# A gated pair of state-space convolutions: the sequence split as 64 rows at stride 32 instead of 32 rows at stride 64, with the transforms in quarter tiles of the matmul array

## The chip, the cores and the metric

The kernel runs on one core of a Trainium2 chip, in float32. The metric is the device time of one execution in microseconds. The core's engines run side by side, each in its own order: TensorE (matmuls, PE in the profile; PEld are its weight loads), VectorE (DVE), ScalarE (ACT), GpSimd (POOL) and SyncE (SP), which issues the transfers. Matmuls read SBUF and write PSUM.

## The reference

Two state-space layers, A and B, are run over the same input and mixed by a gate. Each is a long convolution: a kernel K of 2048 samples for each of 512 channels, made from 128 complex modes, and a causal convolution by a transform of twice the length.

```python
def _A_ref(u, A_re, A_im, B_re, B_im, C_re, C_im, log_dt, Dskip):   # B_ref is the same
    dt = jnp.exp(log_dt)[:, None]
    logdA = dt * (A_re + 1j * A_im)
    dB = dt * (B_re + 1j * B_im)
    P = jnp.exp(logdA[:, :, None] * l[None, None, :])               # l = 0 .. 2047
    K = jnp.einsum("dn,dnl,dn->dl", Cc, P, dB).real
    y = irfft(rfft(pad(u)) * rfft(pad(K)))[..., :L]                 # over the sequence
    return y + u * Dskip
x = A_u
g = sigmoid((x * gate_w).sum(-1, keepdims=True))
return g * a + (1 - g) * b                                          # a = A_ref(x, ..), b = B_ref(x, ..)
```

## The kernel before

The 512 channels are worked in 8 chunks of 64; a chunk holds 128 rows, 64 of layer A and 64 of B. The sequence index is split in two, and the transform is done in two matmul steps with a small transform each, over 32 shifted frequencies of 64 values.

Per chunk there are 8 **tables** (`tables`, T = 0 .. 63 in all), each for 16 rows. GpSimd makes angles (`ang`) and most of the magnitudes (`mr`, some on VectorE), ScalarE takes two sines and a square into PSUM (`s`, `sq`), VectorE multiplies them together (`ei`, `mr`, four instructions). `kgen` (L549, L553) then contracts over the 128 modes on TensorE and gives the convolution kernel in the time domain, with Dskip added to its first sample by the small matmuls of L553. A copy takes the result to `kt`. After each second table `first` (L569) does the first step of the transform in 64x64 tiles; two copies take its two banks to `xa` or `xb`, one buffer for a chunk.

The input's own spectra are made once for pairs of chunks (`u_spectra`: `uin` loads, four `first`, eight steps at L592) and spilled to DRAM (`us`). `gated` makes the gate's matrices `gsi` with a matmul (L613), a tanh and a few small operations.

When a chunk's buffer is full, `conv` runs for it in 8 steps (s = 0 .. 63 in all): two loads of the input's spectrum to `u`, four matmuls of the second step on the full array (L652) into the bank `fw`, one VectorE multiply by `u` (L656) to `y`, eight matmuls of the inverse (L665, L666) into a bank of `c`, a copy to `z` and a spill to `zb` in DRAM. The last chunk's steps use `s` and `sq`, free by then, beside `fw`. After a chunk's 8 steps `fin` loads `zb` back transposed (`f`, in the last chunk `ei` and `mr`), does the inverse's last step together with the gate (L694), copies and stores, four times.

What sets the order: every operation is recorded in program order with its engine or engines, and a table of numbers, `ORDER`, gives the sequence in which they are issued; a letter behind a number picks the second engine. Each engine runs its share strictly in that sequence, and so does the one queue of SP. Rings of buffers (3 of `mr`, 2 of `ei`, `ang`, `u`, `y`, `z`, `f`, one `s` and `sq`; three banks of `c`) set how far one engine may run ahead of another. The prologue (`prep`, `spread_dt`, L366) turns the parameters into the tables' seeds, for the first chunk alone and then for the others in two groups.

A matmul of the program shows in the trace as two records, each with its weight load.

Of the kernel before, what the change touches and what calls it, by code (L numbers as in the profile page):

```python
# [16 lines left out]

L, D, NS = 2048, 512, 128
L1, L2 = 32, 64
F1, F2 = 32, 64  # L20
DC = 64
CU = DC // 4
# [3 lines left out]
NG = CH // G  # L26
QK = CH // 4
GROUPS = ((0,), (1, 2, 3), (4, 5, 6, 7))
# [6 lines left out]
ROUND64 = 1.5 * 2.0 ** 17  # L35


def constants():

    f32 = np.float32  # L40
    out = {}
    l1, f1 = np.arange(L1), np.arange(F1)
    ang = 2 * np.pi * ((l1[:, None] * (4 * f1[None, :] + 1)) % 128) / 128
    c, s = np.cos(ang), np.sin(ang)
    w1k = np.zeros((2, 2, L1, 2, F1, 2))
    for q in range(2):
        w1k[:, q, :, 0, :, q] = c
        w1k[:, q, :, 1, :, q] = -s
    si = np.zeros((F1, 2, 2, 2, L1))
    for q in range(2):  # L50
        si[:, 0, q, q, :] = c.T
        si[:, 1, q, q, :] = -s.T
    l2, f2 = np.arange(L2), np.arange(F2)
    k = l2[None, :, None] * (4 * f1[:, None, None] + 1 + 128 * f2[None, None, :])
    ang = 2 * np.pi * (k % 8192) / 8192
    c, s = np.cos(ang), np.sin(ang)
    w2 = np.concatenate([np.concatenate([c, -s], 2), np.concatenate([s, c], 2)], 1)
    out["w2"] = np.ascontiguousarray(w2.transpose(1, 0, 2)).reshape(128, F1 * 128).astype(f32)

    order = np.array([16 * (2 * r + q) + i for q in range(2) for r in range(2) for i in range(16)])  # L60
    ct = c.transpose(0, 2, 1)[:, :, order] / L
    st = s.transpose(0, 2, 1)[:, :, order] / L
    vv = np.concatenate([np.concatenate([ct, st], 2), np.concatenate([-st, ct], 2)], 1)
    vv = np.concatenate([-vv[:, :, 64:], vv], 2)
    out["vv"] = np.ascontiguousarray(vv.transpose(1, 0, 2)).reshape(128, F1 * 192).astype(f32)
    sign = np.repeat([1.0, -1.0], 64)[:, None]
    out["small"] = np.concatenate([w1k.reshape(128, 128), si.reshape(128, 64), si.reshape(128, 64) / 2, si.reshape(128, 64) / 2, np.eye(128), sign, np.ones((128, 128)), np.full((128, 1), math.pi / 4)], 1).astype(f32)
    ints = np.concatenate([2 * np.arange(32) + 1, np.arange(4), 4 * np.arange(8), [-63]])
    out["cint"] = np.broadcast_to(ints.astype(np.int32), (128, 45)).copy()
    return out  # L70
# [9 lines left out]
30 46 31 176 175 334 185 86 47 178 89 48 13 32 77 14 87 4 33 60 59 179 88 181 61 34 78 91 90 92 35b 93 62b 80 51 180 99 52 79  # L80
53b 66b 70 65b 94 186 56 63 101 95 85 57b 213 54 58 67b 55 81b 333 187b 12 96 102 182 372 71 64 72 217 359 184b 188 183 360
201 100 363 195 103 104 97 124 68 106 69 98 361b 110 189 202 73 364 196 203 362b 198 197 116 107 109 192 365 366 115b 120 16
17 373 117 190 417 204 191 111 367 205 368 376 335 206 105 112b 118 108 113 374b 199 377 127 128 369 375 1321 378 126 119 370
379 380 193b 194 74 125 371b 381 75 388 382 114 383 1328 390b 384 123 385 389 76 122 121 391b 392 129 130 164 387 393 207 133
1322 132b 395 386 358 338 131 210 200 208 135 209 134 136 337 145 137 394 139 146 138 396 401 140 403 402 143 405 144 339 404b
147 141 150 142 148 151b 397 154 211 153 160 398 159b 418 408 399 341 409 155 421 156 406 161 152 407 162 163b 157 400 410 342
212 419b 340 166 170 336 214 422 420 411 168 430 423 424 1335 412 1329 431 216 425 221 165 432 426 434 435 427 9 433b 413 436
414 446 437 475 459 215b 438 447 343 439 149 415b 158 440 416b 460 167 1336 461b 428 462 450 344b 346 218 448 225 220 449b 429
171 451 222 219b 476 345 453 452 441 479 169 224 172 442 454 223b 443 480 463 455 477 456 444 445 482 226 466 464 457 228 227b
478 465 467 232 458b 481 468 235 233 483 484 229 469 234 493 470 485 230b 495 487 231 471 486 472 488 236 494 489 241 237 474  # L90
496 473 490 244 497 509 1323 498 242b 500 243 510 491 245 1324 511 499 246 250 501 1342 1330 247 513 502 512 251 522 492b 514
516 517 503 252 238 523 248 1325 515 249 524 253 1331 504 1326b 525 518 1337 505 526 538 1343 1327 519 540 239 506 1338 527
240 1332 1349 529 528 541 1350 1356 1344 530 507 539 531 1339 551 508 542 1345 532 552 543 520 1340 544 1333 533 1357 1377 569
# [54 lines left out]


class Plan:  # L150

    SWITCH = {"act": 1283, "pe": 100}

    def __init__(self, slots):
        self.slots = slots  # L160
# [36 lines left out]
def ssm_mix(ctx: ExitStack, tc: tile.TileContext, a, out, dry=False):  # L197
# [36 lines left out]
    for k in range(4):  # L234
        single["w2", k] = [128, 8, 128]
        single["vv", k] = [128, 8, 192]
# [547 lines left out]
```

## Time and profile before

| what | value |
|---|---|
| three runs | 506.87, 507.98, 508.52 us, median 507.98 |
| profiled execution, first to last instruction | 507.3 us, mean granted TensorE clock 0.946 |
| instructions in the trace | 23,878 |
| moved by DMA | 86.28 MB, mean 170 GB/s |
| HBM read, written | 53.08 MB, 31.65 MB |

The page splits the time by engine (busy time, share of the span), follows the chain of waits back from the last instruction, and groups instructions by line of the program. Busy time of matmuls is modelled from overlapping records, so how fast TensorE gets on is better read from when its records start. "Issue" in the chain is time in which an engine waited for nothing that the profile names. The instructions themselves also come by DMA; they have queues of their own in the page (q8 and q14).

The forty slices of the span, in tenths of each slice:

```profile
PE   2674467698998986999989798899898989899955
DVE  5999899589899986798879869888998889885420
PEclk9987675989999999999999999999999999999997
DMA  8645754835335754455565635445556769642865
```

### The profile page before, as it was taken

The numbers are of one execution on the slowest core, as the hardware profiler recorded it, in microseconds if no ns is written. First come the engines' busy times: TensorE is split into PE (matmuls) and PEld (weight loads), VectorE is DVE, ScalarE is ACT, GpSimd is POOL, SyncE is SP. The second block draws the span as 40 slices with busy tenths as digits, with TensorE's granted clock in tenths as the row PEclk, the third lists the DMA queues.
The fourth block names the chain that finished last, engine by engine and source line by source line (L and its number), as shares of the span: only waits on it lengthen the run. The fifth ranks groups of instructions, "written<-read, shape, count | busy, mean of one in ns | idle before, by whom it ended". The sixth has DMA issues, their size and how long they took to land.

```text
span 507.3 us, 23878 instructions
## 1 busy us (share of the span) xinstructions
PE 420.6 (83%) x10566; PEld 392.4 (77%) x10566; DVE 413.3 (81%) x526; ACT 366.9 (72%) x630; POOL 367.9 (73%) x302
## 2 busy tenths in 40 slices
PE   2674467698998986999989798899898989899955
PEld 2374456598988885898979798898898889799944
DVE  5999899589899986798879869888998889885420
ACT  3982468878799777798986679788988998762200
POOL 1465449989798998789979968799899989830001
PEclk9987675989999999999999999999999999999997
DMA  8645754835335754455565635445556769642865
GB/s 267 235 148 155 239 137 143 300 130 179 97 97 144 215 171 134 132 174 170 152 185 179 189 107 169 150 147 170 151 168 183 216 184 248 173 127 64 241 191 143
DMA packets 90535, 86.28 MB, mean 170 GB/s; under 512 B 6048, under 2 KB 76832, under 8 KB 90432
## 3 DMA queue, kind: packets, MB, share of 16 engines
q1 hardware_dynamic: 90192, 84.10, 55.6%
q8 instruction: 83, 1.36, 1.1%
q0 software_dynamic: 240, 0.66, 0.4%
q14 instruction: 20, 0.16, 0.1%
HBM read 53.08 MB, written 31.65 MB: 167 GB/s over the span
## 4 chain that ended last, share of the span: by engine, by line
PE 54%; DVE 13%; issue 9%; ACT 8%; DMA 7%; SPq 1%; POOL 0%; POOLq 0%; DVEq 0%; ACTq 0%
PE c L665 10%; PE fw L652 9%; PE c L666 9%; PE c L549 9%; PE c L569 7%; PE c L694 4%; PE c L592 3%; DMA zb<-z 3%; DVE ei L283 3%; DVE mr L293 2%; DMA ei<-zb 1%; DVE y L656 1%; ACT sq L296 1%; DMA gsi<-in_par_dram 1%; ACT ml L489 1%
## 5 line engine op out<-in xcount | busy, mean ns | idle before, releaser
L293 DVE SCALAR_TENSOR_TENSOR mr<-sq,mr 128x1024 f32<-128x1024 f32 (+1 forms) x128 | 118.4, 946 | 6.4 <-ACT sq L296 6.2
L283 POOL TENSOR_TENSOR mr<-ml 128x1024 f32<-128x1024 f32 x55 | 108.3, 1972 | 19.5 <-PE c L549 8.3
L665 PE MATMUL c<-y,vv 128*128 128x128 f32 x512 | 103.5, 284 | 1.9 <-DVE xb L308 1.1
L666 PE MATMUL c<-y,vv 128*128 128x128 f32 x512 | 100.7, 279 | 0.0
L283 POOL TENSOR_TENSOR ang<-par,cint 128x512 int32<-128x512 int32 x64 | 69.4, 1084 | 28.9 <-ACT sq L296 23.0
L283 DVE TENSOR_TENSOR ei<-s,mr 128x1024 f32<-128x1024 f32 x64 | 77.8, 1216 | 8.9 <-PE c L553 4.6
L665 PEld LDWEIGHTS c<-y,vv 128*128 128x128 f32 x512 | 79.0, 195 | 3.4 <-DVE xb L308 1.3
L666 PEld LDWEIGHTS c<-y,vv 128*128 128x128 f32 x512 | 79.3, 196 | 0.0
L296 ACT ACTIVATE s<-ang 128x1024 f32<-128x1024 int32 x64 | 65.9, 1030 | 17.5 <-DVE ei L293 8.4
L656 DVE TENSOR_TENSOR y<-fw,u 128x1024 f32<-128x1024 f32 x57 | 69.3, 1215 | 10.2 <-PE fw L652 9.0
L549 PE MATMUL c<-mr 128*32 128x64 f32 x2048 | 67.0, 227 | 11.8 <-DVE mr L293 7.8
L296 ACT ACTIVATE sq<-ang 128x1024 f32<-128x1024 f32 x64 | 65.9, 1030 | 12.4 <-DVE mr L293 11.7
L306 ACT ACTIVATE z<-c 128x512 f32<-128x512 f32 x73 | 43.1, 591 | 38.8 <-PE c L666 27.3
L283 POOL TENSOR_TENSOR ang<-sa 128x512 int32<-128x512 int32 x64 | 70.0, 1095 | 0.4
L296 ACT ACTIVATE ang<-ang 128x1024 f32<-128x1024 int32 x64 | 67.5, 1054 | 0.7
L549 PE MATMUL c<-ei 128*32 128x64 f32 x2048 | 65.5, 225 | 0.3 <-issue 0.3
L549 PEld LDWEIGHTS c<-mr 128*32 128x32 f32 x2048 | 48.9, 113 | 19.4 <-issue 10.6
L283 POOL TENSOR_TENSOR mr<-mh 128x512 f32<-128x512 f32 x58 | 63.6, 1097 | 0.2
L549 PEld LDWEIGHTS c<-ei 128*32 128x32 f32 x2048 | 50.7, 114 | 0.4 <-issue 0.4
L569 PE MATMUL c<-small,kt 64*64 64x64 f32 x2048 | 43.2, 228 | 8.5 <-issue 5.7
L569 PEld LDWEIGHTS c<-small,kt 64*64 64x64 f32 x2048 | 37.0, 140 | 13.0 <-issue 6.6
L569 PE MATMUL c<-small,uin 64*64 64x64 f32 x1024 | 24.9, 243 | 24.1 <-DMA small<-in_small_dram 7.9
(109 smaller groups left out, 759.8 us busy)
## 6 DMA issues: line engine op xcount, KB each, us to landing
zb<-z SPq DMA_DIRECT2D x64, 256.0 KB, 3.3
u<-us SPq DMA_DIRECT2D x114, 128.0 KB, 3.4
f<-zb SPq DMA_DIRECT2D x28, 512.0 KB, 5.0
us<-z SPq DMA_DIRECT2D x32, 256.0 KB, 2.5
uin<-in_uk_dram SPq DMA_DIRECT2D x16, 256.0 KB, 3.8
f<-in_ut_dram SPq DMA_DIRECT2D x8, 512.0 KB, 5.0
out_dram<-o SPq DMA_DIRECT2D x27, 128.0 KB, 2.7
vv<-in_vv_dram SPq DMA_DIRECT2D x4, 768.0 KB, 8.1
```

Of the source, the lines that this page charges most:

```text
L283: op(engs, 0, lambda e: (dve if e == "dve" else pool).tensor_tensor(out=out(), in0=in0(), in1=in1(), op=o), reads, writes, port=port)
L293: lambda _: dve.scalar_tensor_tensor(out=out(), in0=in0(), scalar=s, in1=in1(), op0=o0, op1=o1), reads, writes, port=port)
L296: op("act", c_act(n), lambda _: act.activation(out=out(), in_=in_(), func=func, **{k: v() if callable(v) else v for k, v in kw.items()}), ...
L306: act.activation(out=o(), in_=i(), func=AF.Copy)
L549: pe.matmul(ps[32 * j:32 * j + 32, o, 0:64], x[:, 4 * o + j, 64:96], x[:, 4 * o + j, 0:64], start=o + part == 0, stop=False, tile_position ...
L569: pe.matmul(t(*ps[h]).rearrange("p a b -> p (a b)")[64 * r:64 * r + 64, 64 * g:64 * g + 64], t(*x)[64 * h:64 * h + 64, g], t("small")[64 * ...
L592: pe.matmul(p[:, k], t("w2", j // 2)[:, 4 * (j % 2) + k], t(*x1)[:, 4 * j + k], start=True, stop=True)
L652: pe.matmul(fv()[:, :, k], t("w2", j // 2)[:, 4 * (j % 2) + k], t(*x1)[:, 4 * j + k], start=True, stop=True)
L656: op("dve", 1134, lambda _: dve.tensor_tensor(out=t(*y).rearrange("p h s f d -> p h s (f d)"), in0=fv().rearrange("p s f d -> p s (f d)"). ...
L665: pe.matmul(t(*ps)[:, k], v[:, 64:192], t(*y)[:, 0, :, k], start=True, stop=False)
L666: pe.matmul(t(*ps)[:, k], v[:, 0:128], t(*y)[:, 1, :, k], start=False, stop=True)
L694: pe.matmul(t(*ps)[64 * r:64 * r + 64, i, 0:DC], t("gsi")[:, 4 * k + i, s, 64 * r:64 * r + 64], fv()[:, r, i, DC * s:DC * s + DC], start=s ...
```

## The change

The sequence is split the other way, 64 rows at stride 32, so there are 64 shifted frequencies of 32 values. Every matmul of the transforms now contracts over 64 rows (real and imaginary parts of 32 values, or 64 samples), and the array is used as quarter tiles, two row halves by two column halves, each half of the rows writing a bank of its own.

- `kgen` swaps the operands: 64 + 2 matmuls a table, 32 wide, instead of 32 + 4, 64 and 4 wide.
- `first` has 64 matmuls on 64 rows and 32 columns instead of 32 on 64 rows and 64 columns, still 64 wide.
- the second step (`spectrum`, for the input and for `conv`) handles 16 frequencies in 32 matmuls, 64x64, 64 wide; there were 4 matmuls of 128x128, 128 wide, a step; 8 steps a chunk are now 4.
- the inverse has 32 matmuls, 64x64, 128 wide, in each of 4 steps a chunk, instead of 8 of 128x128 in each of 8.
- `fin` and the gate keep their matmuls.
- VectorE's multiply takes two instructions a step, one a bank; `u` is loaded by one transfer that writes its rows twice; `us` rows are 2 KB, `f` rows 4 KB.
- rings: `c` has 4 single banks and `fw` is gone; `kt` 2, `z` 3, `u` 2.
- `ORDER` is new throughout, and the buffer of a ring is picked by when it comes free. Its rows are numbers:

```diff
-7 0 8 5 82 6 10 11 2 1 173 3 36b 38b 37b 84 83 40b 39b 43 18 177 41b 50 19 42 15 20 21 22 23 174 25 44 26 45b 27 28 29 24 49
+10 0 11 1 5 9 13 17 7 2 8 6 179 3 12 171 82 18 19 20 24 21 4 22 23 25 26 27 28 29 14 30 31 36 16 38 15 37 315 40 316 39 43 50
```

```diff
-L1, L2 = 32, 64
-F1, F2 = 32, 64
+NB, NA = 64, 32
+F1, F2 = 64, 32
...
         def kgen(_):
-            R, I, ps = t(*M), t(*E), t(*kc)
-            for o in range(4):
+            R, I, ps = t(*M), t(*E), t(*kc)[:, 0:256].rearrange("p (o l) -> p o l", o=8)
+            for o in range(8):
                 for x, part in ((R, 0), (I, 1)):
-                    for j in range(4):
-                        pe.matmul(ps[32 * j:32 * j + 32, o, 0:64], x[:, 4 * o + j, 64:96], x[:, 4 * o + j, 0:64],
-                                  start=o + part == 0, stop=False, tile_position=(0, 32 * j))
...
+                    for j in range(2):
+                        for h in range(2):
+                            pe.matmul(ps[64 * j + 32 * h:64 * j + 32 * h + 32, o], x[:, 2 * o + j, 32 * h:32 * h + 32],
+                                      x[:, 2 * o + j, 64:96], start=o + part == 0, stop=h + o + part == 9, tile_position=(0, 64 * j + 32 * h))
+            for j in range(2):
+                pe.matmul(ps[64 * j:64 * j + 32, :, 0], t("small")[:, 320 + 64 * j:352 + 64 * j], t("dsk")[:, T],
+                          start=False, stop=True, tile_position=(0, 64 * j))
...
         def mm(_):
-            for g in range(8):
-                for r in range(2):
-                    for h in range(2):
-                        pe.matmul(t(*ps[h]).rearrange("p a b -> p (a b)")[64 * r:64 * r + 64, 64 * g:64 * g + 64],
-                                  t(*x)[64 * h:64 * h + 64, g], t("small")[64 * h:64 * h + 64, 64 * r:64 * r + 64],
-                                  start=True, stop=True, tile_position=(64 * h, 64 * r))
...
+            for n in range(8):
+                for s in range(2):
+                    for r in range(2):
+                        for j in range(2):
+                            p0 = 32 * (2 * s + r)
+                            pe.matmul(t(*ps[j])[p0:p0 + 32, 64 * n:64 * n + 64],
+                                      t(*x)[64 * j:64 * j + 64, 2 * n + s], t("small")[64 * j:64 * j + 64, 64 * r:64 * r + 64],
+                                      start=True, stop=True, tile_position=(64 * j, p0))
...
+    def spectrum(x1, j, fw):
+        def mm(_):
+            F = [t(*k).rearrange("p (f d) -> p f d", f=8) for k in fw]
+            for k in range(8):
+                for x in range(2):
+                    for s in range(2):
+                        pe.matmul(F[s][64 * x:64 * x + 64, k], t("w2", j)[64 * s:64 * s + 64, 8 * x + k],
+                                  t(*x1)[64 * s:64 * s + 64, 16 * j + 8 * x + k], start=True, stop=True,
+                                  tile_position=(64 * s, 64 * x))
...
-        def fwd(_):
-            for k in range(4):
-                pe.matmul(fv()[:, :, k], t("w2", j // 2)[:, 4 * (j % 2) + k], t(*x1)[:, 4 * j + k], start=True, stop=True)
...
         def inv(_):
-            for k in range(4):
-                v = t("vv", j // 2)[:, 4 * (j % 2) + k]
-                pe.matmul(t(*ps)[:, k], v[:, 64:192], t(*y)[:, 0, :, k], start=True, stop=False)
-                pe.matmul(t(*ps)[:, k], v[:, 0:128], t(*y)[:, 1, :, k], start=False, stop=True)
...
+            for q in range(4):
+                for h in range(2):
+                    for x in range(2):
+                        for e in range(2):
+                            f = 2 * q + e
+                            v = t("vv", j // 2)[64 * x:64 * x + 64, 8 * (j % 2) + f]
+                            pe.matmul(t(*ps[x])[64 * e:64 * e + 64, CH * q:CH * q + CH], v[:, 0:64] if h else v[:, 32:96],
+                                      t(*y)[64 * x:64 * x + 64, h, f].rearrange("p s d -> p (s d)"),
+                                      start=h == 0, stop=h == 1, tile_position=(64 * x, 64 * e))
```

How TensorE's instructions stand, in two places. First its start, before: L569 is `first` on the input, L366 the spreading of dt, L592 the second step for the input.

```order
L569 MATMUL c<-small,uin 64x64 x64
L366 MATMUL c<-ei,small 128x128
L366 MATMUL c<-ei,small 128x384
L366 MATMUL c<-ei,small 128x512
L569 MATMUL c<-small,uin 64x64 x64
L592 MATMUL c<-xb,w_2_135 128x128 x4
```

and after, where the same three are L545, L343 and L562, L594 is the gate and L524 the first table's `kgen`:

```order
L343 MATMUL c<-ei,small 128x128
L343 MATMUL c<-ei,small 128x384
L545 MATMUL c<-small,uin 32x64 x128
L343 MATMUL c<-ei,small 128x512
L594 MATMUL c<-f,gate_w 128x256 x8
L545 MATMUL c<-small,uin 32x64 x128
L562 MATMUL c<-xb,w_0_178 64x64 x32
L562 MATMUL c<-xb,w_1_179 64x64 x32
L594 MATMUL c<-f,gate_w 128x256 x8
L562 MATMUL c<-xb,w_3_181 64x64 x32
L562 MATMUL c<-xb,w_2_180 64x64 x32
L524 MATMUL c<-mr 32x32 x4
```

The spreading of dt now comes ahead of everything, and four `first` of the input (twice x128) and its four second steps stand ahead of the first table.

Second, the end of the last table on TensorE, before: the last rows of `kgen`, `first` on `kt`, and the inverse's first matmuls.

```order
L549 MATMUL c<-mr 32x64 x4
L549 MATMUL c<-ei 32x64 x4
L553 MATMUL c<-dsk,small 32x4 x4
L569 MATMUL c<-small,kt 64x64 x32
L665 MATMUL c<-y,vv_138 128x128
L666 MATMUL c<-y,vv_138 128x128
```

and after, with L545 as `first`, L562 the second step, L642 the inverse and L673 the gated sums:

```order
L524 MATMUL c<-mr 32x32 x4
L524 MATMUL c<-ei 32x32 x4
L527 MATMUL c<-dsk,small 32x8 x2
L545 MATMUL c<-small,kt 32x64 x64
L562 MATMUL c<-xb,w_0_178 64x64 x32
L562 MATMUL c<-xb,w_2_180 64x64 x32
L642 MATMUL c<-y,vv_182 64x128 x32
L642 MATMUL c<-y,vv_183 64x128 x32
L673 MATMUL c<-f,gsi 64x64 x16
L562 MATMUL c<-xb,w_1_179 64x64 x32
```

The same work stands in fewer and longer steps, and each step has more and smaller matmuls: `first` 64 for 32, the second step 32 where 4 stood, the inverse 32 where 8 stood.

More of the change, by code (lines that the diff above doesn't have):

```diff
@@ L58, in constants @@
[L58 to L65, printed above, removed]
@@ L179, in __call__ @@
         deps.discard(i)
-        soft -= deps
-        engs = eng if isinstance(eng, dict) else {eng: ns}
-        self.ops.append((engs, fn, deps, new, table, moves, soft, heat, port))
+        self.ops.append((engs.split(), kind, n, fn, deps, new, table, port))
     def order(self):
@@ L552, in kgen @@
-            for j in range(4):
-                pe.matmul(ps[32 * j:32 * j + 32, :, 0], t("small")[:, 320 + 32 * j:352 + 32 * j], t("dsk")[:, T],
-                          start=False, stop=True, tile_position=(0, 32 * j))
-        op("pe", 1068, kgen, [M, E, ("dsk",), ("small",)], [kc, kt], table="narrow", heat=(0.74, 0.88))
-        copy(256, lambda: t(*kt)[:, 4 * (T % 2):4 * (T % 2) + 4], lambda: t(*kc)[:, :, 0:64], [kc], [kt])
+                    for j in range(2):
+                        for h in range(2):
+                            pe.matmul(ps[64 * j + 32 * h:64 * j + 32 * h + 32, o], x[:, 2 * o + j, 32 * h:32 * h + 32],
+                                      x[:, 2 * o + j, 64:96], start=o + part == 0, stop=h + o + part == 9, tile_position=(0, 64 * j + 32 * h))
@@ L704, in ssm_mix @@
     load("cint")
-    load("small", 650)
+    load("small", 290)
     load("gate_w")
```

534 lines of the change are left out of this document (259 added, 275 removed), and 25 rows, old and new, of the table ORDER.

## The prediction

> **What bounds the kernel now.** I read the page first, then the busy time by stage, then the places where TensorE stops for nothing that the profile names, and last the end of the chain of waits.
>
> From the page: TensorE's busy row, the chain's shares, and the queue that brings instructions (packets, MB, share of 16 DMA engines).
> ```profile
> PE 420.6 (83%) x10566; PEld 392.4 (77%) x10566; DVE 413.3 (81%) x526; ACT 366.9 (72%) x630; POOL 367.9 (73%) x302
> PE 54%; DVE 13%; issue 9%; ACT 8%; DMA 7%; SPq 1%; POOL 0%; POOLq 0%; DVEq 0%; ACTq 0%
> q8 instruction: 83, 1.36, 1.1%
> ```
> The busy table by stage (stretch, length, then busy us and count of PE, PEld, DVE, ACT, POOL, the granted clock, DMA).
> ```profile
> core 0: us, PE busy (x) PEld busy (x) DVE busy (x) ACT busy (x) POOL busy (x), PEclk, DMA share, GB/s
> 50.00:105.00 55.00, 35.34 (x870) 30.92 (x864) 45.80 (x60) 37.24 (x67) 40.13 (x30) 0.72 0.64 202
> 105.00:200.00 95.00, 84.77 (x2226) 79.72 (x2229) 84.27 (x98) 77.82 (x118) 83.72 (x65) 1.00 0.50 150
> 200.00:300.00 100.00, 92.29 (x2376) 87.33 (x2366) 84.63 (x102) 79.87 (x142) 84.58 (x69) 0.97 0.54 159
> 300.00:400.00 100.00, 91.85 (x2616) 86.29 (x2618) 90.53 (x107) 87.64 (x152) 90.51 (x71) 1.00 0.54 162
> 400.00:440.00 40.00, 36.21 (x1009) 34.23 (x1001) 35.74 (x43) 33.63 (x61) 35.92 (x29) 1.00 0.81 221
> ```
> From 105 us on TensorE is busy 89 to 92%, VectorE 85 to 91%: TensorE leads, VectorE and GpSimd are close behind. So far a change that takes matmul time away looks good. But 9% of the chain is "issue": TensorE waited for nothing that is shown. Two such stops, in the timeline of TensorE's matmuls (start, length, operation, count, idle before):
> ```profile
> 315.79 0.74 PE L569 MATMUL c<-small,uin 64*64 64x64 f32 x33
> 317.56 0.34 PE L569 MATMUL c<-small,uin 64*64 64x64 f32 x6 [1.03 <-issue]
> 319.98 0.85 PE L569 MATMUL c<-small,kt 64*64 64x64 f32 x41
> 321.83 0.38 PE L569 MATMUL c<-small,kt 64*64 64x64 f32 x9 [1.00 <-issue]
> ```
> They fall inside one operation, between matmuls with no semaphore. How often, in the table of waits (us in total, times, longest):
> ```profile
> PE c L569 <- issue: 12.1, 9, 2.5
> PE c L553 <- issue: 6.4, 4, 2.7
> PE c L549 <- issue: 3.8, 5, 1.5
> PE c L694 <- issue: 1.3, 1, 1.3
> ```
> Nineteen stops. Cutting the trace at some of them gives this table (TensorE alone: stretch, length, busy us with the count of matmul records, clock, DMA share, GB/s):
> ```profile
> 189.76:194.03 4.28, 2.81 (x128) 1.00 0.78 227
> 194.03:199.56 5.53, 2.35 (x127) 1.00 0.51 153
> 199.56:209.99 10.43, 9.54 (x255) 0.84 0.18 53
> 314.22:317.56 3.34, 2.27 (x128) 1.00 0.51 123
> 317.56:321.83 4.28, 3.27 (x127) 1.00 0.46 163
> 435.13:439.79 4.66, 3.19 (x128) 1.00 0.57 171
> 439.79:458.94 19.15, 18.31 (x509) 1.00 0.41 117
> ```
> The counts are 128, 255, 509: always a multiple of 128 matmul records, less the odd semaphore instruction. A record has a weight load with it, so 128 records are 256 instructions. Queue q8 brought 1.36 MB in 83 packets, 16.4 KB each; 2 x 10,566 TensorE instructions over 83 are 255. **TensorE's instructions come in blocks of 256, and the stops are at the edges of blocks.** How long a refill takes shows at 457 us: the first row is q8 in the window 456.6 to 457.7, the others the matmuls after it.
> ```profile
> q8 instruction: 1, 0.02, 5.4%
> 457.80 0.31 PE L549 MATMUL c<-mr 128*32 128x64 f32 x7
> 458.94 0.24 PE L549 MATMUL c<-mr 128*32 128x64 f32 x1 [0.84 <-issue]
> ```
> The packet took 5.4% of 16 x 1.1 us = 0.95 us and had landed by 457.7; TensorE went on at 458.94, over 1.2 us later. With the time before the packet starts, one refill is well over 2 us, and no two stops lie closer than 3.34 us. So I take it that the next block is asked for only when the present one is begun: a block costs at least some 3.4 us, however short its matmuls are. Today a block lasts 507.3/83 = 6.1 us on average, so the price mostly hides behind matmul time.
>
> The Trainium skill, page "Runtime: NRT & Kernel Launch", section "Instruction fetch mechanics", has the same blocks (16 KiB, 256 instructions, the next one brought while the present one runs) but says that crossing into a block is mostly hidden. The trace agrees on the size; on "hidden" the stops above differ, and I follow them. What the rule would make of the change is the first rival.
>
> **The change, part by part.** Prices of today's steps, from the chain of waits in order of time (start, length, line, records):
> ```profile
> 447.04 1.02 PE c L549 x62
> 452.25 1.09 PE c L569 x64
> 455.55 0.22 PE c L666 x2
> 462.52 0.89 PE sq L652 x8
> 473.24 2.02 PE c L694 x64
> ```
> Each matmul of the program is two records (10,566 are 2 x 5,283).
>
> Forward transforms over frequencies (L592, L652): now 32 + 64 = 96 steps of 8 records, 0.89 us each, 85 us. After: 16 + 32 = 48 steps of 64 records in 64x64 quarters, the form of L569 today, 1.09 us: 52 us. Inverse (L665, L666): 64 steps of 16 records, 8 x 0.22 = 1.78 us, 114 us; after, 32 steps of 64 records, 128 wide. Four at a time, side by side, they are as many rounds as a step has now: 1.78 us; from L569's 64 records at half that width it would be 2 x 1.09. I take 2.0: 64 us. Saved: 33 + 50 = 83 us of matmul time.
>
> Kernel generation (L549, L553) goes from 72 records, 64 wide, to 132, 32 wide; `first` (L569) from 64 records to 128 on 32 columns. The trace has no such forms. The bounds for a record: today's, 0.11 us for 8 (14 ns); or that of the 4-wide matmuls here,
> ```profile
> 457.06 0.22 PE L553 MATMUL c<-dsk,small 128*32 128x4 f32 x8
> 457.12 0.32 PE L549 MATMUL c<-mr 128*32 128x64 f32 x8
> ```
> eight starts in 0.06 us, 7.5 ns. Half the width is half the streaming, so I take 7.5: 0.99 and 0.96 us a step, about today's 1.07 and 1.09. At 14 ns or, for `first`, 1.09/64 = 17 ns it would be 64 x 0.78 + 48 x 1.09 = 102 us more.
>
> Records now: 64 x 72 + 48 x 64 + 96 x 8 + 64 x 16 + 32 x 32 (the gated sums, L694) + 70 (gate, spreading of dt) = 10,566. After: 64 x 132 + 48 x 128 + 48 x 64 + 32 x 64 + 32 x 32 + 70 = 20,806. **The records double, so the blocks go from 82.5 to 162.5**, and a block's own matmuls shrink: 128 records of kernel generation or `first` are about 1 us, of the forward step 2.2 us, of the inverse and the gated sums 4 us. Most blocks now end long before the next one can be there. The refill, not the array, becomes TensorE's bound. Behind a matmul that waits for its block stand all later ones on TensorE's queue, and for those wait the copies of `kt` on ScalarE, the multiplies `y` on VectorE, and, through the rings of `mr` and `ei` that kernel generation frees, GpSimd.
>
> The price of a block: from below 3.34 us, the shortest stretch in the table; from above 5.53 us, the longest one-block stretch. Between, the five stretches have the median 4.28. They hold 2.3 to 3.3 us of matmuls, so most of each is refill and not work; but the same data bytes will be spread over more time, so packets stand less often in a refill's way. I take 4.15 us.
>
> Everything else goes behind that. The multiplies and evacuations of VectorE and ScalarE keep their element counts (some twenty copies go from VectorE to ScalarE, some ten table products from GpSimd to VectorE); at 413 us the busiest of these engines has far less than TensorE would need. The transfers keep their bytes, `u` loads come in 32 issues instead of 128, `us`, `f` and `u` in longer rows: a small gain that nobody waits for. If that cover were gone, the price is that of the first rival. The new PSUM ring (four single banks for `c`, none for `fw`) lets a two-bank step wait for copies; such waits, like those on the in-order engines, run beside the refills.
>
> **The sum.** TensorE's sequence now begins with the spreading of dt, which needs the same chain as before; its matmuls start between 13.3 and 17.5 us, and I count blocks from 16.6. The end follows the last inverse step:
> ```profile
> L366 PE MATMUL c<-ei,small x6: 422/928/1061, 13.3 to 17.5; 128*128 128x128 f32 x2, 128*128 128x384 f32 x2, 128*128 128x512 f32 x2
> 485.94 0.24 PE c L666 x2
> 486.82 2.43 DMA zb<-z
> 492.14 7.56 DMA ei<-zb
> 499.84 1.66 PE c L694 x32
> ```
> From 485.9 to the end at 507.3 are 21.4 us, which stay (copy, spill, four loads, the last gated sums, stores); one block of records belongs to it. So 16.6 + 161.5 x 4.15 + 21.4 = 708 us of span. The profiled span of before, 507.3, is 0.7 under the median of the runs, 507.98: **709 us**. With 3.34 us a block it is 578, with 4.28 it is 730, with 4.66 it is 791.
>
> The clock adds uncertainty: from 50 to 105 us, with TensorE busy 64%, it was granted 0.72. With refills between, TensorE will be busy less than that, and at half clock the blocks of inverse and gated sums (24 of them, 4 us at full clock) would take 8, up to 24 x 4 = 96 us more if all ran so; blocks of narrow matmuls would still hide behind the refill. I count that to the upper end.
>
> **The rivals.** First, the refill hides, as it does for three of four blocks today (faster). Then the 83 us of matmuls are gone, and the other engines lead: VectorE had 295 us of work in the 335 us from 105 to 440; at 95% that is 311 us, 24 saved, and the eight closing steps of the last chunk go from 8 x 2.67 to 4 x 3.09 us, 9 saved: about 475 us. For it: only 19 of 83 edges cost a visible stop today. Against: those are the edges behind narrow matmuls, the kind that doubles. The refill running further ahead for TensorE than I read is what would bring it about. By the rule of the skill's page the time would be this one.
>
> Second, the refill hides but a narrow record costs what a record costs now: 102 us more against 83 less, 526 us, slower. The point from which it decides is 14 ns a record; the 7.5 ns above speak against it.
>
> Third, the same refill at its floor throughout (under 3.7 us a block, 575 to 635 us): the 3.34 us stretch speaks for it, the three at 4.3 or more against. Fourth, refill plus half clock plus waits on copies, over 790 us.
>
> **Chances.** Refill bound at 3.7 to 4.65 us a block, 635 to 790 us: 0.63, with 709 us as its value. At the floor: 0.17. Over 790: 0.08. First rival: 0.07. Second: 0.05, a fifth of it within what this measurement can tell from no change (0.3%). Range 600 to 790 us: it holds the first and most of the floor case. Faster 0.07, same 0.01, slower 0.92.
>
> **What would show it.** In the profile after: about 163 packets in the instruction queue, 20,806 matmul records; stops named "issue" at every 128 records, all along and not at 20 places; "issue" the largest share of the chain; VectorE under 65% busy; a granted clock well under 0.95. Wrong, if stretches of 128 records run in 1 to 2 us without a stop, or if VectorE is over 85% busy. A step time of 1.8 us for kernel generation without a stop inside would speak for the second rival.

## The result and the profile after

| what | before | after |
|---|---|---|
| median of the runs | 508.25 us (4 runs, 506.87 to 511.38) | 767.57 us (4 runs, 763.43 to 771.93) |
| ratio, 95% interval | | 1.509 (1.501 to 1.517) |
| profiled execution, first to last instruction | 507.3 us | 766.3 us, mean granted clock 0.737 |
| DMA, mean | 170 GB/s | 112 GB/s |

The forecast was 709 us in a range of 600 to 790. The kernel takes half as long again, for the reason forecast, and 58 us longer than the sum said. Some runs of a kernel are a per cent or two slower than its others; medians here are over all its runs, ratios and their intervals over the others alone.

From the page of the changed kernel, the engines' busy row, the instruction queue, the granted clock in 40 slices and the shares of the chain:

```profile
PE 456.1 (60%) x20806; PEld 403.1 (53%) x20806; DVE 424.6 (55%) x501; ACT 384.3 (50%) x666; POOL 349.6 (46%) x287
PEclk9868557867775886557877786558869767777796
q8 instruction: 163, 2.67, 1.5%
PE 52%; issue 28%; DVE 11%; ACT 4%; DMA 4%; POOL 1%; SPq 1%; DVEq 0%; ACTq 0%; POOLq 0%
```

The counts are those of the forecast to the record: 20,806 matmul records, 163 packets of instructions. No engine is over 60% busy, and "issue" went from 9% to 28% of the chain. The table of waits (total us, times, longest) says where it sits; L524 is `kgen`, L545 `first`, L642 the inverse, L562 the second step:

```profile
PE c L524 <- issue: 80.5, 48, 4.2
PE c L545 <- issue: 70.6, 39, 4.7
PE c L642 <- issue: 20.5, 12, 3.2
PE c L562 <- issue: 13.4, 9, 3.8
```

That is 185 us in 108 stops; the four such rows of the kernel before made 23.6 us in 19. Cut at some of the stops, TensorE alone reads (stretch, length, busy us and records, clock, DMA share, GB/s):

```profile
211.93:215.67 3.74, 2.27 (x127) 0.50 0.02 4
247.50:251.50 4.00, 2.08 (x130) 1.00 0.25 70
255.50:259.60 4.10, 4.10 (x128) 0.51 0.21 63
263.14:266.87 3.73, 1.80 (x130) 1.00 0.45 128
266.87:270.59 3.72, 2.69 (x129) 1.00 0.17 54
478.68:482.43 3.75, 2.25 (x129) 0.50 0.18 53
```

Each stretch is one block of 128 records, give or take a few, as the cuts do not fall exactly on its edges. Five of them last 3.7 to 4.0 us, whether their matmuls take 1.8 us or 2.7, at full clock or at half; in the third, half-clock matmuls fill all of 4.1 us. The first and the last row, at half clock, are no longer than the fourth and fifth at full. They also have little data traffic (2% and 18% of the DMA engines), so a block costs some 3.7 us even with almost no transfers beside it.

For all blocks between the first edge and the last I took from the trace when the packet had landed and when the first matmul behind the block's edge started. Where TensorE went on within 1.65 us of the landing, I call the block refill-limited:

```
changed kernel, us        blocks   sum    mean of one
refill-limited               129   527.3   4.09
one pause, 62.99 to 99.75      1    36.8
the tail (spill and load)      1    19.5
the others                    31   163.9   5.29
```

With 13.9 us ahead of the first edge and 4.9 behind the last these make the span, 766.3. (A count moves by two or three with where exactly an edge is put.)

Sorted by the mean busy share of the DMA engines during the block, the 129 are longer the more traffic stands beside them:

```
busy share of the DMA engines   blocks   mean length   packet starts behind the edge (mean)
under 10%                           36      3.68 us      1.16 us
10 to 30%                           23      3.90         1.34
30 to 60%                           49      4.21         1.66
over 60%                            21      4.69         2.30
```

With more transfers under way the packet starts later, and TensorE waits for it. The padded and the first merged kernel below show the same order; no run changed the traffic alone.

The 31 others are not refill-limited. TensorE is busy for 129 of their 164 us, at a mean clock of 0.63 (one of the 31 has over 0.9), and idle for 35, of which all but 1.5 us are waits for copies and products of ScalarE and VectorE.

### The profile page after: what moved, and what is told of

It is laid out like the page before. It is cut to its first block, busy times and chain, and to the rows that moved or that the text cites. A ratio compares the mean times of both kernels' runs of the same rounds, so it can differ in the third digit from the quotient of the medians.

```text
span 766.3 us, 44173 instructions
## 1 busy us (share of the span) xinstructions
PE 456.1 (60%) x20806; PEld 403.1 (53%) x20806; DVE 424.6 (55%) x501; ACT 384.3 (50%) x666; POOL 349.6 (46%) x287
## 4 chain that ended last, share of the span: by engine, by line
PE 52%; issue 28%; DVE 11%; ACT 4%; DMA 4%; POOL 1%; SPq 1%; DVEq 0%; ACTq 0%; POOLq 0%
PE c L524 13%; PE c L642 12%; PE c L545 12%; PE c L562 8%; PE c L673 6%; DVE y L628 1%; DVE gsi L253 1%; DVE mr L263 1%; DVE mr L253 1%; DMA mr<-zb 1%; DMA gsi<-in_par_dram 1%; DVE ei L253 1%; ACT z L276 1%; DVE vv L253 1%; DMA us<-z 1%
## 5 line engine op out<-in xcount | busy, mean ns | idle before, releaser
L524 PE MATMUL c<-mr 128*32 128x32 f32 x4096 | 104.0, 218 | 64.6 <-issue 44.8
L524 PEld LDWEIGHTS c<-mr 128*32 128x32 f32 x4096 | 92.0, 128 | 79.4 <-issue 70.3
L524 PE MATMUL c<-ei 128*32 128x32 f32 x4096 | 103.6, 216 | 35.8 <-issue 35.7
L253 DVE TENSOR_TENSOR ei<-s,mr 128x1024 f32<-128x1024 f32 x64 | 78.2, 1221 | 67.2 <-ACT s L266 36.8
L642 PE MATMUL c<-y,vv 64*64 64x128 f32 x2048 | 97.3, 346 | 26.6 <-issue 20.5
L524 PEld LDWEIGHTS c<-ei 128*32 128x32 f32 x4096 | 93.1, 129 | 35.8 <-issue 35.8
L642 PEld LDWEIGHTS c<-y,vv 64*64 64x64 f32 x2048 | 84.2, 178 | 33.6 <-issue 29.2
L545 PE MATMUL c<-small,kt 64*32 64x64 f32 x4096 | 69.5, 273 | 54.4 <-issue 48.9
L628 DVE TENSOR_TENSOR y<-c,u 128x1024 f32<-128x1024 f32 x58 | 69.3, 1217 | 42.4 <-PE c L562 42.4
L545 PEld LDWEIGHTS c<-small,kt 64*32 64x32 f32 x4096 | 55.5, 128 | 64.1 <-issue 55.5
L562 PE MATMUL c<-xb,w 64*64 64x64 f32 x2048 | 55.2, 274 | 25.1 <-issue 9.6
L562 PEld LDWEIGHTS c<-xb,w 64*64 64x64 f32 x2048 | 49.3, 183 | 29.9 <-issue 9.2
```

Source lines behind the costliest of these rows:

```text
L253: lambda e: (dve if e == "dve" else pool).tensor_tensor(out=out(), in0=in0(), in1=in1(), op=o),
L524: pe.matmul(ps[64 * j + 32 * h:64 * j + 32 * h + 32, o], x[:, 2 * o + j, 32 * h:32 * h + 32], x[:, 2 * o + j, 64:96], start=o + part == 0, ...
L545: pe.matmul(t(*ps[j])[p0:p0 + 32, 64 * n:64 * n + 64], t(*x)[64 * j:64 * j + 64, 2 * n + s], t("small")[64 * j:64 * j + 64, 64 * r:64 * r ...
L562: pe.matmul(F[s][64 * x:64 * x + 64, k], t("w2", j)[64 * s:64 * s + 64, 8 * x + k], t(*x1)[64 * s:64 * s + 64, 16 * j + 8 * x + k], start= ...
L628: op("dve", "tt1", 1024, lambda _, s=s: dve.tensor_tensor(out=t(*y)[:, :, :, s], in0=t(*fw[s]).rearrange("p (f d) -> p f d", f=8).unsqueez ...
L642: pe.matmul(t(*ps[x])[64 * e:64 * e + 64, CH * q:CH * q + CH], v[:, 0:64] if h else v[:, 32:96], t(*y)[64 * x:64 * x + 64, h, f].rearrange ...
```

## The experiments

Eleven kernels. Line numbers shift by a few between them: `kgen` is L549, L550 or L553/L554 (the Dskip matmuls) in those made from the kernel before, L523 to L534 in those made from the changed one.

**More blocks in the kernel before.** Three kernels leave the old split, order, rings and transfers as they were and only give `kgen` more records. The first:

```diff
-    pe.matmul(ps[32 * j:32 * j + 32, o, 0:64], x[:, 4 * o + j, 64:96], x[:, 4 * o + j, 0:64],
-              start=o + part == 0, stop=False, tile_position=(0, 32 * j))
+    for h in range(2):
+        pe.matmul(ps[32 * j:32 * j + 32, o, 32 * h:32 * h + 32], x[:, 4 * o + j, 64:96], x[:, 4 * o + j, 32 * h:32 * h + 32],
+                  start=h + o + part == 0, stop=False, tile_position=(0, 32 * j))
```

> The kernel before, with each 64-wide matmul of kgen cut into two 32-wide ones on the same stationary operand: the same arithmetic, 128 + 8 records a table instead of 64 + 8, so 14,662 records in all and 114.5 blocks of instructions instead of 82.5. Refill theory (each 128 records of TensorE cost one fetched block, about 4.1 us when their matmuls are shorter than that): 113.5 x 4.1 + 38 us of head and tail = 503 us is about what the kernel takes already, so only the unevenness of the blocks costs: 520 to 560 us, with clearly more stops at block edges than 19. Array theory (narrow matmuls are slow in themselves, blocks do not matter): 136 records at 8.7 ns are 1.18 us a table instead of 1.07, 7 us in all: 508 to 515 us, stops as now.

Measured 616.2 us, ratio 1.212 (1.204 to 1.220): 108 us for 32 blocks, 3.4 each.

The second is the same with `range(4)` and 16 columns.

> The kernel before, with each 64-wide matmul of kgen cut into four 16-wide ones: the same arithmetic, order, rings and transfers, 256 + 8 records a table, 22,854 in all, 178.5 blocks. Refill theory: 177.5 x 4.1 + 38 = 766 us, the time of the changed kernel. Array theory: 264 records at 8.7 ns are 2.30 us a table instead of 1.07, 79 us in all: 587 us at most. Order theory (the changed kernel is slow by its new order, rings and loads): none of that is in here, so 508 to 587 us.

Measured 880.3 us (864.1 to 884.4). The third issues the Dskip matmuls 16 times:

```diff
-            for j in range(4):
-                pe.matmul(ps[32 * j:32 * j + 32, :, 0], ..., start=False, stop=True, ...)
+            for n in range(16):
+                for j in range(4):
+                    pe.matmul(ps[32 * j:32 * j + 32, :, 0], ..., start=False, stop=n == 15, ...)
```

> The kernel before, with the four 4-wide Dskip matmuls of each table issued 16 times (the Dskip term is added 16 times over): 120 records more a table that do almost no work, 18,246 records, 142.5 blocks. Refill theory: 141.5 x 4.1 + 38 = 618 us. Array theory: 120 records at 7.5 ns are 0.9 us a table, 58 us: 566 us at most. Order theory: 508 to 566 us.

Measured 743.9 us, ratio 1.466 (1.457 to 1.475): 236 us for 60 blocks, 3.9 each, although these records do almost no work. From its page and its table of waits:

```profile
PE 568.7 (77%) x18246; PEld 534.4 (72%) x18246; DVE 416.4 (56%) x526; ACT 369.7 (50%) x630; POOL 367.7 (50%) x302
q8 instruction: 143, 2.34, 1.3%
PE c L554 <- issue: 95.4, 48, 3.4
```

The stops now sit in the Dskip matmuls, at 48 places. The array theory and the order theory, at most 566 us both, are out. The refill theory's own figures were too low each time (766 and 618 us), and so was 520 to 560 for the split in two: they counted every block at 4.1 us. In the kernel with 142.5 blocks 74 are refill-limited, of 3.84 us, but the other 68, with the wide matmuls in them, still last 6.4 on average. An added block comes on top of those.

In the split in four, four matmuls in a row go to the same column tile, and they start some 20 ns apart on average, not 8.7. So it was run again with the tiles in turn:

```diff
+    for h in range(4):
+        for j in range(4):
+            pe.matmul(ps[32 * j:32 * j + 32, o, 16 * h:16 * h + 16], x[:, 4 * o + j, 64:96], x[:, 4 * o + j, 16 * h:16 * h + 16],
```

> The kernel before with each 64-wide matmul of kgen cut into four 16-wide ones, this time in turn over the four column tiles, so that no tile gets two matmuls in a row (the earlier split gave four in a row to one tile, and its records came 26 ns apart by the median instead of 7). 22,854 records, 178.5 blocks, 96 more than before. Refill theory: 96 blocks at the 3.4 to 3.9 us that the 32 and the 60 added blocks of the earlier runs cost: 834 to 882 us less what the earlier split's array time put on top, so 780 to 880 us. Array theory: 264 records at 8.8 ns are 2.3 us a table instead of 1.07, 80 us in all: 588 us.

Measured 887.8 us, ratio 1.743 (1.733 to 1.753): 379 us for 96 blocks, 3.95 each, 8 us above the range of the refill theory. One stretch of `kgen` in each of the two kernels, TensorE alone (columns as above), first four in a row to one tile, then the tiles in turn:

```profile
109.08:111.00 1.92, 1.92 (x109) 1.00 0.88 212
```

```profile
81.09:81.93 0.84, 0.84 (x100) 1.00 0.56 68
```

The records run more than twice as fast in the second kernel, and its time did not fall: 887.8 us. The Trainium skill, page "TensorE: Matmul & The Clock Gate", section "Back-to-back issue gap", gives a floor of about 25 ns between matmuls of up to 64 columns. The trace agrees in part for matmuls on one tile: the median gap in that kernel is 26 ns, but gaps of 4 to 7 ns stand between, so the first stretch has 18 ns a record. With four tiles in turn it shows 8.4 ns, so here there is no such floor for the array as a whole.

**Fewer blocks in the changed kernel.** `kgen` with one 64-column operand for two of 32; the Dskip matmuls become 64 columns wide with it:

```diff
-                        for h in range(2):
-                            pe.matmul(ps[64 * j + 32 * h:64 * j + 32 * h + 32, o], x[:, 2 * o + j, 32 * h:32 * h + 32],
-                                      x[:, 2 * o + j, 64:96], ...)
+                        pe.matmul(ps[64 * j:64 * j + 64, o], x[:, 2 * o + j, 0:64], x[:, 2 * o + j, 64:96], ...)
```

> The changed kernel, with kgen's two 32-column stationary operands taken as one of 64 columns: half as many matmuls in kgen, 64 + 4 records a table instead of 128 + 4, the same arithmetic, order, rings and transfers; 16,710 records, 130.5 blocks instead of 162.5. Refill theory: 767 - 32 x 4.1 = 636 us. Array theory: at most 64 records at 8.7 ns a table fall away, 36 us: 731 us or more. Half clock theory (TensorE is slow since its clock is 0.74): no less than 731 us either. Order theory: about 767 us.

Measured 686.8 us, ratio 1.348 (1.338 to 1.359): 81 us less than the changed kernel, between the theories. A stretch of `kgen` in the changed kernel, and one of the merged kernel:

```profile
219.41:220.27 0.86, 0.86 (x101) 1.00 0.47 171
```

```profile
139.91:141.76 1.85, 1.85 (x72) 1.00 0.41 156
```

With only two tiles to alternate, records start 29 ns apart on average (66 in 1.9 us) instead of 8.7 (132 in 1.15 us). So a table gets 0.77 us dearer on the array, 49 us for 64 tables. 32 blocks at 4.09 less 49 us is 82, close to what was measured; but this sum was made after the result, and no run parts its two terms. That the 49 us would show in full was not expected; it fits that only 84 of the 131 blocks here are refill-limited.

Then `first` too, merged in the same way:

```diff
-                for s in range(2):
-                    for r in range(2):
-                        for j in range(2):
-                            pe.matmul(t(*ps[j])[p0:p0 + 32, 64 * n:64 * n + 64], t(*x)[64 * j:64 * j + 64, 2 * n + s], ...)
+                for r in range(2):
+                    for j in range(2):
+                        pe.matmul(t(*ps[j])[64 * r:64 * r + 64, 64 * n:64 * n + 64], t(*x)[64 * j:64 * j + 64, 2 * n:2 * n + 2]..., ...)
```

> The changed kernel with kgen merged as in the run before and also first: two 32-column stationary operands taken as one of 64, half as many matmuls (its halves then land on other rows, so the output is not the reference's; the amount of work, the order and the rings stay). 13,638 records, 106.5 blocks. Refill theory: 24 blocks fewer than the run with kgen merged alone (686.8 us) at 3.4 to 4.1 us: 589 to 605 us. Array theory: first takes 64 records at 17 ns (1.09 us) instead of 128 at 10 (1.28), 9 us in all: 678 us.

Measured 616.7 us, ratio 1.206 (1.197 to 1.214): 70 us for 24 blocks, 2.9 each, against 9 in all by the array theory and 82 to 98 by the refill theory. Only 44 of the 107 blocks left are refill-limited, so a block taken away gives less than 4 us.

**Work added to the array.** A wide matmul ahead of every `kgen` and `first`, in the changed kernel and in the one before:

```diff
+            pe.matmul(t(*kc), t("small")[:, 320:448], t(*M).rearrange("p a b -> p (a b)")[:, 0:512], start=True, stop=True)
             for o in range(8):
...
+            pe.matmul(t(*ps[0]), t("small")[:, 320:448], t(*x).rearrange("p a b -> p (a b)")[:, 0:512], start=True, stop=True)
             for n in range(8):
```

> The changed kernel with one 128x128 matmul of 512 columns put ahead of every kgen and every first, into the bank that the next matmul overwrites: 112 such matmuls, 224 records more (1.75 blocks). Their array time, from the 0.22 us of two 128-wide records at full clock and the 0.33 us of one 256-wide record of the gate, is 0.88 to 1.3 us each, 99 to 146 us in all. Refill theory: 129 of the changed kernel's 162 blocks end before the next one has been fetched, so four fifths of this work runs in time that TensorE waits anyway; 7 us for the blocks and 20 to 30 us for the rest: 775 to 805 us, with a higher clock. Array theory (or half clock: TensorE's own work sets the time): 866 to 913 us.

> The control for the run above: the same 112 matmuls of 512 columns in the kernel before, 99 us at its full clock. Only 22 of its 82 blocks end before the next one has been fetched, so by the refill theory most of the work shows: 75 to 110 us, 583 to 618 us. If wide matmuls were cheap for another reason (VectorE or GpSimd set the pace), much less: 510 to 540 us.

Measured in the changed kernel 789.4 us, ratio 1.557 (1.540 to 1.574), 22 us more; in the kernel before 568.3 us, ratio 1.125 (1.113 to 1.138), 60 us more. The groups by form show the added matmuls (records, busy us, mean ns of one), and the pages the busy row and the granted clock; first the changed kernel:

```profile
L520 PE MATMUL c<-mr,small 128*128 128x512 f32 x128 | 85.6, 755 | 24.7 <-DVE mr L263 12.9 <-ACT z L276 5.5 <-issue 3.6
L541 PE MATMUL c<-kt,small 128*128 128x512 f32 x64 | 41.1, 728 | 6.6 <-ACT kt L276 4.7 <-DVE kt L278 1.2 <-ACT xa L276 0.7
L541 PE MATMUL c<-uin,small 128*128 128x512 f32 x32 | 21.5, 760 | 24.4 <-ACT gsi L276 24.4
PE 523.2 (67%) x21030; PEld 378.4 (48%) x21030; DVE 427.2 (55%) x501; ACT 383.2 (49%) x666; POOL 350.8 (45%) x287
PEclk9888589899978898986998999998989789989995
```

then the kernel before:

```profile
L546 PE MATMUL c<-mr,small 128*128 128x512 f32 x128 | 68.9, 621 | 5.0 <-DVE mr L293 5.0
PE 510.3 (90%) x10790; PEld 407.5 (72%) x10790; DVE 416.9 (74%) x526; ACT 369.2 (65%) x630; POOL 367.8 (65%) x302
PEclk9879779999999999999999999999999999999996
PE 75%; DVE 8%; DMA 5%; ACT 3%; issue 2%; POOLq 0%; POOL 0%; SPq 0%; DVEq 0%; ACTq 0%
```

148 us of matmuls were added to the changed kernel, and 22 show. The added work also raised its mean clock from 0.737 to 0.879, and the kernel's own matmuls got shorter for it, so TensorE's busy time rose by only 67 us, from 456.1 to 523.2. A third of that shows; the rest ran while TensorE would have waited. Its refill-limited blocks (130, of 4.06 us) got no shorter at the higher clock. In the kernel before the busy time rose by 90 us, from 420.6 to 510.3, and 60 of them show, two thirds. That is less than expected: there the padding itself hid the refills ("issue" fell from 9% to 2% of the chain, and 6 of 84 edges are refill-limited instead of 22).

**The pause at 63 us.** TensorE stands still for one long stretch in the changed kernel (TensorE alone, and from the waits):

```profile
62.99:99.75 36.76, 6.92 (x153) 0.67 0.45 124
```

```profile
PE c L545 <- ACT gsi L276: 23.1, 1, 23.1
```

`first` needs two of the four banks of `c`. They are held by the gate, whose copies to `gsi` wait until the preparation of the later chunks' parameters has left `gsi`. The chain of waits there is that preparation, on VectorE:

```profile
66.14 7.41 DMA gsi<-in_par_dram
78.12 3.19 DVE gsi L253
86.20 3.26 DVE gsi L419
99.07 0.61 DVE gsi L278
99.72 0.31 PE c L545
```

The experiment moves the gate's last two groups behind the preparation and six blocks' worth of `first` and `kgen` ahead of it; only rows of the order change (numbers of the table; b picks the second engine):

```diff
-... 389 391 428 392 416 415 417 393 119 418 ...
+... 389 391 428 392 416 415 417 393 208 210b 209b 216 211 217b 218b 394 395 367 369 368 410 411 396 397b 398b 119 418 ...
```

> The changed kernel with rows of its order moved: the last two of the gate's four matmul groups (with their loads) go behind the preparation of the later chunks' parameters, and six blocks' worth of TensorE's work (two first of the second pair's input, two tables' kgen and two first on kt, 776 records) goes ahead of it, into the 36.8 us in which the changed kernel's TensorE stands still at 63 to 99.8 us. Refill theory: that pause is no refill, it is a price of the order of its own, and filling it with six blocks of about 4.1 us gives back 20 to 25 us: 742 to 747 us, with as many blocks as before (163). Order theory (the order and its waits carry most of the loss): well over 50 us come back, under 715 us, since the tables start earlier. If the engines behind the pause set the time anyway: 767 us.

Measured 776.1 us, ratio 1.524 (1.516 to 1.531): no gain. The pause went elsewhere:

```profile
63.80:85.37 21.57, 11.52 (x640) 0.58 0.28 80
85.37:125.32 39.95, 13.24 (x128) 0.55 0.39 127
```

The copies of the moved steps stood on VectorE ahead of the preparation, each waiting for a block of TensorE, and the preparation ended 25 us later. So the same once more with the copies on ScalarE, spread among its own steps (no b behind the numbers, and `394 395` behind 136, `367 369 368 410` behind 457, `411 396` behind 142, `397 398` behind 153).

> As the run with the gate moved, but the moved steps' copies go to ScalarE and are spread among its steps of the parameters' preparation, so that VectorE's chain of preparation is not queued behind them (there the chain, and with it the pause, came 25 us later: the pause moved to 85.4 to 125.3 us and the time stayed). Refill theory: VectorE's chain ends near 99 us again and six blocks are done by then: 742 to 752 us. If other engines set the time from there on: 760 to 770 us.

Measured 754.3 us (750.1 to 759.8), ratio 1.493 (1.477 to 1.509). What is left of the pause in that kernel:

```profile
91.81:107.80 15.99, 11.21 (x154) 0.71 0.62 207
```

21 us of the pause are gone and the median is 13 us lower. The interval overlaps the changed kernel's (1.501 to 1.517), so a gain is likely, but neither it nor its size is settled.

**A version of the kernel before with fewer blocks.** The one thing the study offered for beating both kernels: the four Dskip matmuls of a table as one.

```diff
-            for j in range(4):
-                pe.matmul(ps[32 * j:32 * j + 32, :, 0], t("small")[:, 320 + 32 * j:352 + 32 * j], t("dsk")[:, T], ...)
+            pe.matmul(ps[:, :, 0], t("small")[:, 320:448], t("dsk")[:, T], start=False, stop=True)
```

> The kernel before with the four 4-wide Dskip matmuls of a table taken as one on the full array: 2 records instead of 8 a table, 384 fewer, 3 blocks fewer; all else as before. Refill theory: 3 blocks at 2 to 4 us, 6 to 12 us: 496 to 502 us. Array theory: 6 records at 8 ns a table, 3 us: 505 us, or slower than 508 us if going from quarter tiles to the full array and back costs more than 0.05 us each time.

Measured 520.3 us, ratio 1.012 (1.005 to 1.019): no gain, by the ratio 2 to 10 us slower, with 80 packets instead of 83. Two rows of its chain show a likely reason (start, length, line, records):

```profile
233.66 1.03 PE c L549 x64
234.69 0.32 PE c L552 x2
```

The Dskip matmuls of a table in the kernel before, in its chain, and the inverse's first matmuls behind them:

```profile
299.21 0.05 PE c L553 x7
299.26 0.42 PE c L665 x2
299.68 0.22 PE c L666 x2
```

One matmul on the whole array holds the chain for 0.32 us where the four on quarter tiles held it for 0.05; it seems to wait until the tiles ahead of it are empty, which no run shows by itself. The inverse's first pair, on the whole array too, takes 0.42 us behind the quarter tiles instead of 0.22, so where it follows, part of that wait was there already. 0.27 us for 64 tables is at most 17 us, more than three blocks can give back where only a quarter of the edges is refill-limited.

## Why the prediction was right, and where its sum was not

**The mechanism** stands. Blocks of 256 instructions are the bound: records that do almost nothing cost 3.9 us per 128 in the old order and with the old rings (236 us for 60 blocks), and of 67 us by which padding raised TensorE's busy time in the changed kernel 22 show. The Trainium skill, page "Runtime: NRT & Kernel Launch", section "Instruction fetch mechanics", calls crossing into a block mostly hidden; by that the time would have been near 475 us, and it is 767.6. Here the trace decides against the sentence: a crossing is hidden only where the block ahead has some 4 us of work.

**The price of a block**, 4.15 us, was close: 129 refill-limited blocks have a mean of 4.09 and a median of 3.86. The reason given for a price under the 4.28 of before, thinner traffic, is borne out: the DMA engines are busy for 34% of the time in these blocks on average and for 62% in the refill-limited ones of the kernel before, and the table above goes from 3.68 us to 4.69 with the traffic. One reading under it was wrong: in four of the five stretches matmuls fill two thirds or more of the time (2.81 of 4.28 us, say), so "most of each is refill and not work" does not hold; work and refill run side by side, and the refill sets the length. Nor is 3.34 us a least price: two blocks of the changed kernel took under 2 us (1.75 behind the pause, 1.97 behind a block of 5.87), since the next packet had started before their first matmul.

**The step that failed** is "161.5 x 4.15" as the whole of the middle: it took every block for a refill, and everything else for hidden behind it. 31 blocks are not refill-limited and average 5.29 us, which is (5.29 - 4.15) x 31 = 35 us. One holds the pause, 36.8 - 4.15 = 33 us. The refill-limited ones gave 8 back. That is 60 us, and the time missed by 58.

What makes the 31 long is the waits for ScalarE and VectorE (33 us in them) and the half clock; the inverse of one takes 3.69 us at a clock of 0.50, against 1.91 at full clock in a row further down:

```profile
337.48 3.69 PE c L642 x64
```

No run parts the two.

The pause has its words in the prediction: waits on the new ring of `c`, "like those on the in-order engines, run beside the refills". They do not where one engine's chain is longer than the refills beside it; and the price was in the order, which shows the gate ahead of the first table. By 105 us the kernel before had made seven tables, the changed one three (these rows are the half of `kgen` that reads `mr`: 32 records a table before, 64 after):

```profile
L549 PE MATMUL c<-mr 128*32 128x64 f32 x224 | 9.6, 268 | 7.8 <-DVE mr L293 7.8
```

```profile
L524 PE MATMUL c<-mr 128*32 128x32 f32 x198 | 5.3, 228 | 3.2 <-ACT z L276 2.0 <-issue 0.7 <-ACT kt L276 0.5
```

**The prices of the matmuls.** From the chain of the changed kernel at full clock:

```profile
248.22 1.09 PE c L562 x64
384.06 1.91 PE c L642 x64
436.70 1.18 PE c L673 x32
```

The second step is 1.09 us as forecast, the inverse 1.91 (2.0). The narrow forms were taken at 7.5 ns a record; they are 8.7 in `kgen` and 9.8 in `first` at full clock, so 1.15 and 1.25 us a step instead of 0.99 and 0.96, 24 us of array time in all. By the padded kernel such time shows to about a third (22 of 67 us), some 8 us, as an estimate. The 83 us that the transforms save were there at full clock only: at the clock granted TensorE's busy time rose, from 420.6 to 456.1 us.

**The half clock** was counted to the upper end with up to 96 us. It came (0.737). In the refill-limited blocks it shows no cost: they have a median of 3.75 us at half clock and 3.89 at full, and work added in the waits brought the clock back to 0.879 without making them shorter (a block whose matmuls the half clock draws out past its refill is not among them). In the 31 others, at 0.63 on average, it costs a part of the 35 us above, which was not measured apart.

**The ends.** The first edge came at 13.9 us (16.6 assumed). The last inverse is done at 742.30 us, and from there to the end at 766.3 are 24.0 us, against 21.4. The rows to compare with those of before, from the end of the chain:

```profile
740.02 2.28 PE c L642 x64
...
748.65 8.08 DMA mr<-zb
...
756.83 3.70 PE c L673 x64
```

**The rivals.** The first (refill hidden) and the second (narrow records at today's price) fell with the Dskip run. The third, the floor under 3.7 us a block, was met by 34 of the 129 blocks, not by their mean; of the five stretches it was argued from, four and not three are at 4.28 us or more. The fourth, over 790 us, named the right kinds of extra cost and put them too high. Of what was to show it, all came but one: "issue" is not the largest share of the chain, TensorE's matmuls are (52% against 28%), because the chain counts the matmuls of a block up to its stop, and in five of the six stretches above those fill 1.8 to 2.7 us of some 3.7 to 4.0. Of the signs of being wrong, stretches of 1 to 2 us without a stop, the two blocks named above are the only ones.

## What to carry to other kernels

Count TensorE's instructions, not only its array time: here 128 records with their weight loads are one fetched block, and a run of blocks with less than about 4 us of work each goes at 4 us a block. Quarter tiles that halve a matmul double the blocks, so here they would pay only where wide matmuls in the same block cover the fetch. And a pause that one engine's chain sets is not filled by moving another engine's work into it, if that work's copies stand on the first engine's queue.

## What was not expected of the hardware

- Starts of matmul records depend on the tiles in turn: on average 8.4 to 8.7 ns over four column tiles of 32, 29 ns over two of 64 columns, 18 to 20 ns with four matmuls in a row, 16 wide, on one tile of 32.
- A single matmul on the full array behind quarter tiles held the chain for 0.32 us, for 2 records 4 wide.
- The granted clock followed the padding, 0.737 to 0.879, and the refill-limited blocks kept their length (4.09 and 4.06 us).
- Three parts of a refill show: in the changed kernel the packet starts some 1.2 us after the block before it has begun (the median), takes 1.1 us, and TensorE goes on some 1.4 us after it has landed. Of the 129 refill-limited blocks 84 have the packet under way within 1.5 us and average 3.69 us; in 15 it starts over 2.9 us late, and they take 5.3 to 7.6. The later starts go with more data traffic.
